# Aligning the heads of four instruction streams to fetch blocks in a single-core decode kernel

## Chip, cores and metric

One core of one Trainium2 chip. The metric is the device time of one execution in microseconds (us); before the change it was 437.0 us, the median of three runs (436.9 to 437.09). Engines are named as in the profile: PE (TensorE), DVE (VectorE), ACT (ScalarE), POOL (GpSimd), SP (SyncE). A fetch is here a packet on one of the DMA queues that the profile marks "instruction" (16 KB or 8 KB each in the trace of before), and a fetch block is the piece of an instruction stream that one such packet is taken to carry.

## What the kernel must compute

One decode step of a conditioned transformer block, batch 8, bf16:

```python
mod = silu(c) @ w_mod                                  # c 8x1024, w_mod 1024x6144; six vectors sa ca ga sb cb gb
h = layernorm(x) * (1 + ca) + sa
x = x + ga * attention(h, k_cache, v_cache, wq, wo)    # 32 query heads, 4 KV heads, 8192 keys, head size 128
h = layernorm(x) * (1 + cb) + sb
x = x + gb * (relu(h @ W_gate) * (h @ W_up)) @ W_down  # 1024 -> 3584 -> 1024
```

K and V are 134.2 MB of the 185.6 MB that must be read.

## The kernel before

A small scheduler, `Prog`, collects the operations of each engine with what they read and write, works out the semaphore waits, and emits one instruction stream for each engine. SP issues all large loads into a ring in on-chip memory. DVE and PE run the attention as a hardware loop of eight trips, two tiles of K and V (4 MB each) to a trip; ACT and POOL are unrolled.

```python
def emit(self, nc, engines, sems):
    ...
    def straight(x, ops):                 # code outside the loop
        known, off = state[x]
        for o in ops:
            want = {}
            ...                           # which semaphores, which values
            body(x, o, new)               # the waits, then the instructions

    after = {}
    for x in engines:                     # sp, act, pool, dve, pe
        mine = [i for i, o in enumerate(self.ops) if o["eng"] == x]
        inside = [i for i in mine if self.ops[i]["trip"] is not None]
        after[x] = [self.ops[i] for i in mine if inside and i > inside[-1]]
        straight(x, [self.ops[i] for i in mine if not inside or i < inside[0]])
        ...
    with nc.Fori(0, len(self.trips["pe"]), engines=...):   # DVE and PE only
        ...
```

The operations at the start, shortened:

```python
pump()                                                  # SP: first half of w_mod, 6 MB
for t, src in enumerate((c_rows, x_rows)):              # 16 KB each: c on SP's queue, A_x on ACT's
    P.op("sp" if t == 0 else "act", lambda e, t=t, src=src: e.dma_start(cx[:, t, :], src), ...)
pump()                                                  # SP: second half of w_mod, Wq, ...
P.op("pool", memset identf); P.op("pool", affine_select identf); ...; rsel; ones; qpad; pT; oT; hmT; identb
P.op("pe", matmul rsel x cx)                            # PE's first matmul: waits for c, A_x and rsel
```

and the tail: `lu = down * gate` and `ob = lu + x` on DVE, then two stores of `ob`.

By count of the built program (the trace does not show it), ACT has 73 instructions, POOL 90, DVE 112 and PE 1351; the loop is PE's instructions 306 to 586.

## Time and profile before

| | before |
|---|---|
| time, median of 3 | 437.0 us |
| span in the profile | 435.9 us |
| moved from HBM | 185.63 MB |
| one loop trip (two K and two V tiles) | about 38.7 us |

The first fence is from the page: the DMA engines in 40 equal slices of the span (a digit is the busy share in tenths, 9 is 90% or more; GB/s is what they moved), and the DMA queues with packets, MB and their share of the 16 DMA engines' span.

```profile
span 435.9 us, 3952 instructions
...
DMA  9999999999999999999999999999999999999995
GB/s 367 435 447 436 432 433 433 432 430 433 433 433 433 433 433 433 431 433 433 433 433 433 433 433 433 433 431 433 433 433 433 433 433 433 426 433 444 421 425 233
...
q1 hardware_dynamic: 6848, 185.63, 98.9%
q8 instruction: 5, 0.08, 0.1%
...
q14 instruction: 3, 0.02, 0.0%
```

The DMA engines are busy throughout, and one queue, q1, which carries the loads, has nearly all of it. The queues marked "instruction" are read here as the fetches of instruction blocks: five packets of 16 KB on q8 and three of 8 KB on q14. The single packet records of the trace put them at 46.2, 86.5, 389.5, 401.9 and 429.8 us (16 KB, 0.88 to 0.95 us each) and at 86.7, 177.6 and 292.8 us (8 KB, 0.31 us each).

Next, the start in order of time (start, duration, engine, line, operation; in brackets the idle time before and what ended it). "SPq" and "ACTq" are issues of loads.

```profile
0.51 0.42 SPq L409 DMA_DIRECT2D cx<-in_c_dram  x1
0.73 0.20 POOL L419 MEMSET identf<- 128x128 f32 x1 [0.29 <-POOLq L812]
0.75 0.39 ACTq L409 DMA_DIRECT2D cx<-in_A_x_dram  x1
...
1.16 1.28 ACT L439 ACT_TABLE_LOAD   x1 [1.16 <-PEq L812]
...
17.69 0.60 PE L435 MATMUL ps<-cx,rsel 32*128 32x512 bf16 x1 [17.69 <-DMA cx<-in_c_dram]
```

ACT issues A_x at 0.75 us and goes on to its table load at 1.16. PE's first matmul waits until c has landed, 17.69 us.

The windows view gives for each stretch its length, the busy time of each engine with the number of instructions, the granted PE clock, the DMA share and GB/s. The first row is the time just before the loop, with Wq arriving; the second is a loop trip.

```profile
core 0: us, PE busy (x) PEld busy (x) DVE busy (x) ACT busy (x) POOL busy (x), PEclk, DMA share, GB/s
...
36.00:48.00 12.00, 3.45 (x32) 0.58 (x16) 2.34 (x5) 0.00 (x0) 0.00 (x0) 0.72 0.97 419
...
100.70:139.40 38.70, 28.11 (x141) 12.40 (x138) 29.75 (x40) 2.56 (x6) 1.64 (x8) 0.85 1.00 434
```

Last, a row of the view of waits (who waited for what: us in total, times, longest).

```profile
DVE kt L575 <- DVEq L180: 30.6, 16, 2.8
```

L575 is the transpose of K, and L180 is the wait ahead of it. All 16 of these waits are at the first transpose of a K tile.

### The profile page before, as it was taken

To read this page: it belongs to the slowest core of one execution; us is meant where nothing else is said; L and a number is where in the kernel's file an instruction comes from. 1 tells how busy PE (TensorE), PEld (TensorE's weight loads), DVE (VectorE), ACT (ScalarE), POOL (GpSimd) and SP (SyncE) were. 2 spreads that over 40 slices of the span, in tenths; PEclk is the share of its full clock that TensorE was granted. 3 is DMA by queue.
4 is the path that set the end of the run, shared out by engine and by line. 5 is a ranking of instruction groups with operands and counts; after the bars stand their busy time and mean duration, and the time that the engine had idled before them with its cause. 6 is when DMAs were issued, how large, how long until landed. Compare 5 with 4: busy or idle time off the path is not lost.

```text
span 435.9 us, 3952 instructions
## 1 busy us (share of the span) xinstructions
PE 275.6 (63%) x1697; PEld 120.4 (28%) x1537; DVE 265.4 (61%) x376; ACT 30.7 (7%) x65; POOL 20.9 (5%) x79
## 2 busy tenths in 40 slices
PE   0063248668595957759595866859595785656336
PEld 0010012323242332324242332324233232352005
DVE  0233048678686877777696867868687777233020
ACT  1100020010101011010101011010101101010000
POOL 7000010000000000000000000000000000000000
PEclk9997658698887889697896969888798969666858
DMA  9999999999999999999999999999999999999995
GB/s 367 435 447 436 432 433 433 432 430 433 433 433 433 433 433 433 431 433 433 433 433 433 433 433 433 433 431 433 433 433 433 433 433 433 426 433 444 421 425 233
DMA packets 6936, 185.76 MB, mean 426 GB/s; under 512 B 816, under 2 KB 912, under 8 KB 1168
## 3 DMA queue, kind: packets, MB, share of 16 engines
q1 hardware_dynamic: 6848, 185.63, 98.9%
q8 instruction: 5, 0.08, 0.1%
q10 hardware_dynamic: 80, 0.02, 0.0%
q14 instruction: 3, 0.02, 0.0%
HBM read 185.63 MB, written 0.02 MB: 426 GB/s over the span
## 4 chain that ended last, share of the span: by engine, by line
PE 46%; DVE 20%; issue 13%; DMA 7%; ACT 0%; SPq 0%
PE ps L634 21%; PE ps L586 18%; DVE kt L575 9%; DMA arena<-in_B_W_down_dram 7%; DVE negm L598 5%; PE ps L604 2%; PE ps L651 2%; PE ps L762 1%; PE ps L731 1%; DVE om L645 1%; DVE mj L609 1%; DVE mjt L612 1%; DVE negm L602 1%; DVE kt L721 0%; DVE lx L693 0%
## 5 line engine op out<-in xcount | busy, mean ns | idle before, releaser
L575 DVE STREAM_TRANSPOSE kt<-arena 128x1024 uint32<-128x1024 uint32 x128 | 149.6, 1217 | 36.8 <-DVEq L180 30.6
L586 PE MATMUL ps<-kt,qpad 128*128 128x512 bf16 x512 | 121.8, 384 | 9.5 <-DVE kt L575 8.2
L634 PE MATMUL ps<-arena,pT 128*64 128x512 bf16 x512 | 93.1, 543 | 50.8 <-issue 50.8
L634 PEld LDWEIGHTS ps<-arena,pT 128*64 128x64 bf16 x512 | 44.9, 155 | 92.8 <-issue 87.5
L586 PEld LDWEIGHTS ps<-kt,qpad 128*128 128x128 bf16 x512 | 45.8, 97 | 83.9 <-DVE kt L575 30.1
L625 DVE STREAM_TRANSPOSE pT<-prb 64x1024 bf16<-64x1024 bf16 x32 | 39.7, 1239 | 16.7 <-ACT prb L618 16.1
L618 ACT ACTIVATE prb<-ps,bias 128x1024 bf16<-128x1024 f32 x16 | 17.8, 1114 | 286.8 <-DVE mjt L612 286.8
L598 DVE TENSOR_REDUCE negm<-ps 128x1 f32<-128x512 f32 x32 | 22.1, 692 | 12.2 <-PE ps L586 12.2
L568 POOL COPY qpad<-qR 32x32 bf16<-32x32 bf16 x64 | 13.1, 204 | 307.7 <-DVE mjt L612 254.3
L762 PE MATMUL ps<-arena,hT 128*32 128x448 bf16 x128 | 12.3, 570 | 10.8 <-DMA arena<-in_B_W_up_dram 5.5
L645 DVE SCALAR_TENSOR_TENSOR om<-ps,im,om 128x128 f32<-128x128 f32 x51 | 17.7, 347 | 0.7
L651 PE MATMUL ps<-jmp,om 128*128 128x16 f32 x34 | 6.9, 280 | 17.0 <-DVE om L645 17.0
L604 PE MATMUL ps<-identf,negm 128*128 128x128 f32 x32 | 7.8, 326 | 15.6 <-DVE negm L602 15.6
L522 PE MATMUL ps<-arena,hT 128*32 128x512 bf16 x64 | 7.1, 620 | 14.6 <-DMA arena<-in_A_wq_dram 14.6
L769 DVE TENSOR_TENSOR kt<-ps,kt 128x448 bf16<-128x448 f32 x2 | 1.2, 620 | 22.0 <-PE ps L762 22.0
L781 PE MATMUL ps<-arena,hmT 128*32 128x256 bf16 x112 | 8.2, 307 | 6.1 <-DMA arena<-in_B_W_down_dram 6.1
L437 DVE CAST cxr<-ps 128x512 bf16<-128x512 f32 x1 | 0.7, 693 | 18.3 <-PE ps L435 18.3
L435 PE MATMUL ps<-cx,rsel 32*128 32x512 bf16 x1 | 0.6, 604 | 17.7 <-DMA cx<-in_c_dram 17.7
L532 DVE CAST kt<-ps 128x512 bf16<-128x512 f32 x1 | 0.7, 692 | 18.1 <-PE ps L522 18.1
L604 PEld LDWEIGHTS ps<-identf,negm 128*128 128x128 f32 x32 | 4.7, 186 | 23.5 <-DVE negm L602 23.5
L651 PEld LDWEIGHTS ps<-jmp,om 128*128 128x128 f32 x34 | 5.3, 195 | 20.5 <-DVE om L645 20.5
L781 PEld LDWEIGHTS ps<-arena,hmT 128*32 128x32 bf16 x112 | 6.0, 109 | 9.2 <-DMA arena<-in_B_W_down_dram 8.1
(88 smaller groups left out, 98.2 us busy)
## 6 DMA issues: line engine op xcount, KB each, us to landing
arena<-in_A_k_cache_dram SPq DMA_DIRECT2D x16, 4096.0 KB, 25.0
arena<-in_A_v_cache_dram SPq DMA_DIRECT2D x16, 4096.0 KB, 20.7
arena<-in_w_mod_dram SPq DMA_DIRECT2D x2, 6144.0 KB, 24.2
arena<-in_A_wq_dram SPq DMA_DIRECT2D x2, 4096.0 KB, 30.6
arena<-in_A_wo_dram SPq DMA_DIRECT2D x2, 4096.0 KB, 23.1
arena<-in_B_W_gate_dram SPq DMA_DIRECT2D x2, 3584.0 KB, 20.9
arena<-in_B_W_up_dram SPq DMA_DIRECT2D x2, 3584.0 KB, 23.3
arena<-in_B_W_down_dram SPq DMA_DIRECT2D x1, 3584.0 KB, 23.7
```

Of the source, the lines that this page charges most:

```text
L568: P.op("pool", lambda e, n=2 * m + Q // 2, Q=Q: e.tensor_copy(qpad[32 * Q:32 * Q + 32, m % 2, :, 24 + 32 * Q:32 + 32 * Q], qR[32 * Q:32 * ...
L575: P.op("dve", lambda e: e.transpose(ktb[:, to:to + QE].bitcast(dt.uint32), arena[:, lo:lo + QE].bitcast(dt.uint32)), reads=[slot_r(lo, lo ...
L586: fns.append(lambda e, t=t, r=r: e.matmul(ps[:, b, :].rearrange("p (c k) -> p c k", k=32), qpad[:, m % 2, t * 2 + r, 24 - 8 * i:152 - 8 * ...
L598: P.op("dve", lambda e: e.tensor_reduce(negm[:, h:h + 1], ps[:, b, :], AX.X, ALU.max, negate=True), reads=[bank(b)] + (free(("v", m - 1)) ...
L604: P.op("pe", lambda e: e.matmul(ps[:, 4, 0:128], negm[:, 2:3].to_broadcast([128, 128]), identf[:], start=True, stop=True), reads=[R("negm" ...
L618: P.op("act", lambda e: e.activation(prb[:], ps[:, 2 * z:2 * z + 2, :].rearrange("p h n -> p (h n)"), ACT.Exp, bias=bias[:, z:z + 1], scal ...
L625: P.op("dve", lambda e, g=g: e.transpose(pT[64 * g:64 * g + 64, z, :, g, :], prb[64 * g:64 * g + 64, :]), reads=[R("prb"), R("pT", z, z + ...
L634: fns.append(lambda e, t=t: e.matmul(ps[64 * (t % 2):64 * (t % 2) + 64, 5, :].rearrange("p (i d) -> p i d", d=Dh), pT[:, z, t].rearrange(" ...
L645: P.op("dve", lambda e, i=i: e.scalar_tensor_tensor(out=om[:], in0=ps[:, 5, Dh * i:Dh * i + Dh], scalar=im[:, i:i + 1], in1=om[:], op0=ALU ...
L651: P.op("pe", lambda e: e.matmul(ps[:, 6 + z, 0:16], om[:], jmp[:].rearrange("p g j -> p (g j)"), start=True, stop=True), reads=[R("om"), R ...
L762: fns.append(lambda e, w=w, r=kk - r0, kk=kk, h=h, j=j, b0=b0: hold(e.matmul(ps[32 * j:32 * j + 32, b0 + h, 0:H], hT[:, kk, :], w[:, r, j, ...
L781: fns.append(lambda e, w=w, r=k - r0, k=k, i2=i2, j=j: e.matmul(ps[32 * j:32 * j + 32, 4, 0:256], hmT[:, k, 1 - i2:33 - i2], w[:, r, i2, j ...
```

## The change

```diff
--- before.py
+++ after.py
@@ -20,6 +20,7 @@
 
     ENGINES = ("sp", "act", "pool", "dve", "pe")
     LOOPED = ("dve", "pe")
+    ALIGNED = dict(act=128, pool=128, dve=128, pe=256)
     N_DMA_SEMS = 20
 
     def __init__(self):
@@ -59,7 +60,7 @@
         self.segs[name] = out
         return covered
 
-    def op(self, eng, fns, reads=(), writes=(), dma=False, own=None, own_wait=None):
+    def op(self, eng, fns, reads=(), writes=(), dma=False, own=None, own_wait=None, page=False):
         if callable(fns):
             fns = [fns]
         i = len(self.ops)
@@ -77,7 +78,7 @@
                 if s[2] is not None and not readers:
                     deps.add((s[2], "waw"))
                 s[2], s[3] = i, []
-        o = dict(eng=eng, fns=fns, writes=list(writes), deps=deps, dma=None, own=own, own_wait=own_wait,
+        o = dict(eng=eng, fns=fns, writes=list(writes), deps=deps, dma=None, own=own, page=page, own_wait=own_wait,
                  trip=self.trip if eng in self.LOOPED else None)
         if dma:
             o["dma"] = self.n_dma
@@ -191,6 +192,10 @@
         def straight(x, ops):
             known, off = state[x]
             for o in ops:
+                if o["page"]:
+                    name = "page_%d" % len(pages)
+                    engines[x].br(name).branch_hint(pages.pop())
+                    nc.switch_bb(name)
                 want = {}
                 for d in o["waits"]:
                     p = self.ops[d]
@@ -203,7 +208,12 @@
                 body(x, o, new)
 
         after = {}
+        pages = []
         for x in engines:
+            if x in self.ALIGNED:
+                engines[x].addr_align(self.ALIGNED[x], offset=0, max_nops=0)
+            if x == "pe":
+                pages.extend(engines[x].mark_branch_hint_location() for o in self.ops if o["page"])
             mine = [i for i, o in enumerate(self.ops) if o["eng"] == x]
             inside = [i for i in mine if self.ops[i]["trip"] is not None]
             after[x] = [self.ops[i] for i in mine if inside and i > inside[-1]]
```

No operation of this kernel passes `page=True`, so those hunks emit nothing. What is left is one `addr_align` on each of four engines; the profile counts four instructions more, 3956 instead of 3952, and the trace of the change has one branch more on each: at 0.69 us on POOL, 0.73 on ACT, 0.76 on DVE and 0.82 on PE.

## The prediction

> What bounds the kernel now. A stream of 185.63 MB from HBM. The page's slices show the DMA engines nine tenths busy or more in 39 of 40 slices, and queue q1 has 98.9% of their span; the windows view gives a DMA share of 1.00 and 432 to 434 GB/s in each loop trip from 62 to 333 us. 185.63 MB at 433 GB/s is 428.7 us; the rest of the 435.9 us is the start, the small last loads (351 GB/s from 424 to 432 us) and 3.5 us after the last weights land. In a trip PE is busy 28.1 of 38.7 us, DVE 29.8, and DVE still waits about 2 us per half trip for K (L575 in the waits view, 30.6 us over 16). The 3.17 us "issue" waits before the PV matmuls are no fetch stalls: the exp (1.1 us) and two transposes of p (2.5 us) run in them.

> What the change does. The `page` hunks are dead: no op passes page=True. What is left is one alignment, with a branch, on ACT, POOL, DVE (128 instructions) and PE (256), at the head of the kernel's own code. No compute, wait or data load changes; instruction fetches move. As built before, ACT has 73 instructions, POOL 90, DVE 112, PE 1351: aligned, the first three fit one block each, PE six. The trace shows fetch packets after the start: five of 16 KB for PE (46, 86, 390, 402, 430 us, about 0.93 us each) and three of 8 KB (87, 178, 293 us, 0.31 us each), all overlapped. They fit PE boundaries at its instructions 192, 448, 704, 960, 1216; after: 256, 512, 768, 1024, 1280. The loop (306 to 586) lies over two blocks before and after, and later trips refetch nothing, so there is nothing to gain in it. [...] at worst a fetch of 2 to 4 us (estimate: PE's packets come about 3 us after its crossing).

> Critical path. Even 4 us at the start is hidden: PE's first matmul waits for c until 17.7 us; POOL is done at 8.7; A_x, issued by ACT at 0.75, lands at 10.1. Wq matmuls wait 6.9 us for data, and Wq half 2 (issued at 32) and K (35) are issued some 6 us before the queue would run dry. One more 16 KB packet costs one DMA engine about 0.6 us at 27 GB/s (433/16, estimate): 0.0 to +0.6 us. The last PE packet moves from 430 to about 432 us, beside the last W_down loads: some tenths at most.

> Predicted: 437.1 us, 436.4 to 438.0 in 8 of 10; faster by over 2%: 0.01, within 2%: 0.97, slower by over 2%: 0.02.

> Right if: trips keep 38.7 us and 433 GB/s; the 8 KB packets of 87, 178 and 293 us are gone or at the very start; PE's packets move by a quarter block; PE's first matmul still waits for c near 17.7 us; POOL's and ACT's first instructions come 0.1 to 4 us later. Wrong if: the branch delays DMA issues so that the queue runs dry before 60 us; the loop's new position makes PE or DVE refetch in every trip (14 or more extra packets and a gap over the 2 us slack); or a fetch stalls PE or DVE after 432 us, where nothing hides it.

The forecast of 437.1 us is before's 437.0 us with the term for one more fetch packet (0.0 to +0.6 us) and at most some tenths for the last one. The branch was no term of the sum: the text counts up to 4 us at the start as hidden.

## The result

| | before | after |
|---|---|---|
| median, 6 runs each | 437.13 us | 437.34 us |
| range | 436.9 to 446.54 | 437.28 to 437.46 |
| ratio of fast runs, after over before | | 1.0005, 95% interval 0.9992 to 1.0019 |

A ratio here and below is the mean time of one kernel's fast runs over the mean of the other's fast runs of the same rounds, so it is not quite the ratio of the medians. The one run of before at 446.5 us counts as slow and is left out of it. The time is the same.

The same lines of the page after:

```profile
span 436.0 us, 3956 instructions
...
DMA  9999999999999999999999999999999999999995
GB/s 378 404 445 433 433 431 436 436 433 428 433 433 436 433 433 433 436 433 433 433 433 433 433 433 433 433 433 433 433 436 433 433 433 433 424 443 425 431 420 244
...
q1 hardware_dynamic: 6848, 185.63, 98.9%
q8 instruction: 6, 0.10, 0.1%
...
q14 instruction: 4, 0.02, 0.0%
```

The packet records show what moved. PE's fetches now come at 5.5, 61.3, 104.1, 390.3, 403.0 and 430.8 us: one more than before, and the others at new places. The three 8 KB fetches in mid-run are gone, and three appear at 5.64, 5.71 and 5.76 us. (The page counts four packets on q14; the fourth is one of 96 bytes at 0.15 us, which just fell inside the span.)

The start after (the change adds ten lines, so L409 of before is L419 here):

```profile
0.51 0.42 SPq L419 DMA_DIRECT2D cx<-in_c_dram  x1
...
1.15 0.20 POOL L429 MEMSET identf<- 128x128 f32 x1 [0.71 <-POOLq L822]
1.17 6.87 ACTq L419 DMA_DIRECT2D cx<-in_A_x_dram  x1
...
8.07 1.28 ACT L449 ACT_TABLE_LOAD   x1 [8.07 <-issue]
...
19.42 0.60 PE L445 MATMUL ps<-cx,rsel 32*128 32x512 bf16 x1 [19.42 <-DMA cx<-in_c_dram]
```

Three things are new. POOL starts 0.42 us later (1.15 instead of 0.73 us), and so does ACT. ACT's issue of A_x, though, takes 6.87 us instead of 0.39, so that its table load comes at 8.07 us. And c, which SP issued at the same time as before, lands 1.7 us later, which moves PE's first matmul from 17.69 to 19.42 us.

In the windows, the loop trip is as it was, and the stretch before the loop has the same DMA share within 0.02 (columns as before):

```profile
36.00:48.00 12.00, 4.17 (x44) 0.58 (x16) 3.39 (x7) 0.60 (x1) 0.00 (x0) 0.72 0.99 429
...
100.70:139.40 38.70, 28.06 (x142) 12.47 (x140) 29.39 (x40) 2.56 (x6) 1.62 (x8) 0.85 1.00 432
```

The first K tile is issued at 36.61 us instead of 34.88, but the third at 75.80 instead of 76.11, and the loop's first transpose starts at 62.75 us, against 62.68 before: the 1.7 us were gone before the loop began.

These three novelties leave three questions: what held ACT for nearly 7 us, what made c late, and whether the stream of loads really hides both and whatever the change might do inside the loop.

### The profile page after: what moved, and what is told of

It is laid out like the page before. It is cut to its first block, busy times and chain, and to the rows that moved or that the text cites. A ratio compares the mean times of both kernels' runs of the same rounds, so it can differ in the third digit from the quotient of the medians.

```text
span 436.0 us, 3956 instructions
## 1 busy us (share of the span) xinstructions
PE 275.4 (63%) x1697; PEld 120.6 (28%) x1537; DVE 263.3 (60%) x376; ACT 30.7 (7%) x65; POOL 20.8 (5%) x79
## 3 DMA queue, kind: packets, MB, share of 16 engines
q1 hardware_dynamic: 6848, 185.63, 98.9%
HBM read 185.63 MB, written 0.02 MB: 426 GB/s over the span
## 5 line engine op out<-in xcount | busy, mean ns | idle before, releaser
L644 PE MATMUL ps<-arena,pT 128*64 128x512 bf16 x512 | 91.9, 538 | 50.8 <-issue 50.8
L635 DVE STREAM_TRANSPOSE pT<-prb 64x1024 bf16<-64x1024 bf16 x32 | 39.7, 1239 | 16.7 <-ACT prb L628 16.1
L628 ACT ACTIVATE prb<-ps,bias 128x1024 bf16<-128x1024 f32 x16 | 17.8, 1113 | 286.2 <-DVE mjt L622 286.2
L655 DVE SCALAR_TENSOR_TENSOR om<-ps,im,om 128x128 f32<-128x128 f32 x51 | 17.7, 347 | 0.7
L532 PE MATMUL ps<-arena,hT 128*32 128x512 bf16 x64 | 7.2, 631 | 12.8 <-DMA arena<-in_A_wq_dram 12.8
L445 PE MATMUL ps<-cx,rsel 32*128 32x512 bf16 x1 | 0.6, 602 | 19.4 <-DMA cx<-in_c_dram 19.4
```

The source lines that it names most:

```text
L628: P.op("act", lambda e: e.activation(prb[:], ps[:, 2 * z:2 * z + 2, :].rearrange("p h n -> p (h n)"), ACT.Exp, bias=bias[:, z:z + 1], scal ...
L635: P.op("dve", lambda e, g=g: e.transpose(pT[64 * g:64 * g + 64, z, :, g, :], prb[64 * g:64 * g + 64, :]), reads=[R("prb"), R("pT", z, z + ...
L644: fns.append(lambda e, t=t: e.matmul(ps[64 * (t % 2):64 * (t % 2) + 64, 5, :].rearrange("p (i d) -> p i d", d=Dh), pT[:, z, t].rearrange(" ...
L655: P.op("dve", lambda e, i=i: e.scalar_tensor_tensor(out=om[:], in0=ps[:, 5, Dh * i:Dh * i + Dh], scalar=im[:, i:i + 1], in1=om[:], op0=ALU ...
```

## Experiments

Twelve runs were made, one of them (start_later5_again) a repetition. The two that load only half of most K and V tiles compute on stale data: the check did not notice that. Short fences show A_x's issue, ACT's first table load and PE's first matmul, in that form of the timeline.

| run | median us | ratio to before (95% interval) |
|---|---|---|
| act_only | 437.52 | 1.0006 (0.9985 to 1.0028) |
| pe_only | 436.73 | 0.9995 (0.9977 to 1.0013) |
| act_after_x | 437.06 | 1.0005 (0.9987 to 1.0023) |
| x_late | 437.32 | 1.0017 (0.9997 to 1.0038) |
| act_x_at_8 | 436.99 | 0.9997 (0.9981 to 1.0014) |
| start_later5 | 439.00 | 1.0039 (0.9979 to 1.0099) |
| start_later5_again | 437.82 | 0.9997 (0.9964 to 1.0029) |
| start_later12 | 443.01 | 1.0122 (1.0076 to 1.0169) |
| half_plain | 430.88 | 0.9829 (0.9778 to 0.9879) |
| half_aligned | 430.57 | 0.9831 (0.9787 to 0.9875) |
| tail_one | 437.53 | 1.0012 (0.9995 to 1.0028) |
| tail_three | 442.49 | 1.0124 (1.0107 to 1.0141) |

The medians include slow runs (one of act_only, one of start_later5_again); the ratios do not. By the rule of 2% the verdict is "same" for all but the two half runs, which are "unclear"; start_later12 and tail_three are slower all the same, by 1.2%, with intervals clear of 1.

### act_only: ScalarE alone is aligned

```diff
-    ALIGNED = dict(act=128, pool=128, dve=128, pe=256)
+    ALIGNED = dict(act=128)
```

> Only ScalarE is aligned. After the change ScalarE issued A_x at 1.17 us, that issue took 6.87 us, the table load came at 8.07 and A_x landed 7.5 us later than before; c landed on a few engines 1.7 us late. If ScalarE's own branch causes all this, this run shows the same: issue of A_x near 1.2 us, about 6.9 us long, table load at 8 us. If the fetches of the other engines (PE's 16 KB above all) cause it, ScalarE shows only the branch of 0.4 us and A_x lands near 10 us. Time under both theories within 0.3% of before (about 437.2 us), because data loads bound the kernel.

```profile
1.17 5.92 ACTq L419 DMA_DIRECT2D cx<-in_A_x_dram  x1
...
7.12 1.28 ACT L449 ACT_TABLE_LOAD   x1 [7.12 <-issue]
...
18.04 0.60 PE L445 MATMUL ps<-cx,rsel 32*128 32x512 bf16 x1 [18.04 <-DMA cx<-in_c_dram]
```

In this run ACT's own branch is enough: the issue comes at 1.17 us and takes 5.92 us. One 8 KB fetch packet came at 5.53 us, and the one that before had at 292.8 us is missing, so that one was ACT's. c is late by 0.35 us only (18.04 instead of 17.69). That is small but outside the scatter: in the five profiles with c undisturbed (before, x_late, half_plain, tail_one, tail_three) this matmul starts between 17.57 and 17.72 us.

### pe_only: TensorE alone is aligned

```diff
-    ALIGNED = dict(act=128, pool=128, dve=128, pe=256)
+    ALIGNED = dict(pe=256)
```

> Only TensorE is aligned. One 16 KB fetch packet near 5 us; six such packets in all. If this packet delays c on a few DMA engines, c lands near 19.4 us instead of 17.7; if the late A_x packets of ScalarE's queue do, c lands at 17.7 us. A_x is issued at 0.75 us and lands near 10. Time within 0.3% of before.

```profile
0.75 0.39 ACTq L419 DMA_DIRECT2D cx<-in_A_x_dram  x1
...
1.16 1.28 ACT L449 ACT_TABLE_LOAD   x1 [1.16 <-PEq L822]
...
18.48 0.60 PE L445 MATMUL ps<-cx,rsel 32*128 32x512 bf16 x1 [18.48 <-DMA cx<-in_c_dram]
```

ACT is as before. PE's fetches came at 5.3, 61.2, 103.6, 390.1, 402.7 and 430.4 us, so the q8 packets are PE's. c is late by 0.79 us with nothing else changed: here one more 16 KB fetch packet ahead of it goes with the whole delay. c's 32 packets of 512 bytes show where: 28 of them started between 16.25 and 16.6 us, the last four at 17.4 to 17.7. After the full change 20 of the 32 started by 16.6 us and the last 12 between 16.85 and 18.62. So some of c's packets lag, read here as those of a few of the 16 DMA engines, and PE's first matmul waits for the last of them: of c's 16 landing signals the last came at 17.64 us in before, and after the change the last five came at 18.17 to 19.37 us, with the matmul at 19.42. The expectation of 19.4 us for this run was too high: only the kernels in which all four engines fetch come to 19 us or more (19.02 in act_after_x, 19.42 in the change, 19.61 in half_aligned).

### act_after_x: ScalarE branches after it has issued A_x

```diff
-    ALIGNED = dict(act=128, pool=128, dve=128, pe=256)
+    ALIGNED = dict(pool=128, dve=128, pe=256)
...
-  lambda e: e.dma_start(cx[:, t, :], src)
+  lambda e: (e.dma_start(cx[:, t, :], src), t == 1 and e.addr_align(128, offset=0, max_nops=0))[0]
```

> All four engines are aligned as in the change, but ScalarE branches after it has issued A_x. Theory fetch (ScalarE stands still until its block has come): A_x lands near 10 us, but the table load still comes at 6 to 8 us. Theory order (the issue of A_x is held up because it now comes after the issue of the second half of w_mod at 0.98 us): the issue at 0.75 us takes 0.4 us, and the table load follows within 1 us of it. Time within 0.3% of before either way.

```profile
0.74 0.39 ACTq L419 DMA_DIRECT2D cx<-in_A_x_dram  x1
...
1.58 1.28 ACT L451 ACT_TABLE_LOAD   x1 [1.58 <-SPq L824]
...
19.02 0.60 PE L447 MATMUL ps<-cx,rsel 32*128 32x512 bf16 x1 [19.02 <-DMA cx<-in_c_dram]
```

The issue takes 0.39 us and the table load comes at 1.58 us, 0.42 us later than before: the price of the branch here. It did not wait until 6 to 8 us, as the simple fetch theory had it: that theory falls. c is still late (19.02 us, 1.33 more than before), as the fetch packets are still there (q8 has six, as in the change). The other 0.40 us of the change's 1.73 come only with the late A_x; whether they are its doing or scatter, no run separates.

### x_late: no alignment, A_x issued after the second half of w_mod

```diff
-for t, src in enumerate((c_rows, x_rows)):
+for t, src in enumerate((c_rows,)):
...
 P.op("pool", lambda e: aff(e, identf[:], 0, [[-1, 128]]), ...)
+P.op("act", lambda e: e.dma_start(cx[:, 1, :], xsrc), reads=[R("identf")], ...)
```

> No alignment at all; ScalarE's A_x load waits for GpSimd's identity, ready at 1.5 us, so that it is issued after the second half of w_mod. Theory order: the issue takes about 7 us again and the packets of A_x come after 12 us. Theory fetch: it takes 0.4 us and A_x lands near 10 to 11 us. Time within 0.3% of before.

```profile
1.50 0.39 ACTq L422 DMA_DIRECT2D cx<-in_A_x_dram  x1
...
1.92 1.28 ACT L441 ACT_TABLE_LOAD   x1 [1.92 <-POOL rsel L424]
...
17.68 0.60 PE L437 MATMUL ps<-cx,rsel 32*128 32x512 bf16 x1 [17.68 <-DMA cx<-in_c_dram]
```

Issued at 1.50 us, after the second half of w_mod, the load still took 0.39 us to issue. So the order theory falls as well. With no fetch at the start, c landed as before.

Both first theories are out. What is left, as a theory, is that it needs both: a branch that has just set off a fetch, and then a DMA issue.

### act_x_at_8: ScalarE aligned, A_x issued after the fetch has landed

```diff
-    ALIGNED = dict(act=128, pool=128, dve=128, pe=256)
+    ALIGNED = dict(act=128)
...
 P.op("pool", lambda e: e.memset(oT[:], 0.0), ...)
+P.op("act", lambda e: e.dma_start(cx[:, 1, :], xsrc), reads=[R("oT")], ...)
```

> ScalarE alone is aligned, and its A_x load, still the first instruction of the new block, waits for a GpSimd memset that ends near 7.4 us, after the fetch packet of 5.5 us has landed. Theory overlap (an issue of a DMA right after the branch is held until the fetch that the branch set off is done): the issue now takes 0.4 us and A_x lands near 17 us. Rival, place (the first DMA issue in a new block is slow whenever it comes): it takes 6 us again, from 7.5 to 13.5 us. Time within 0.3% of before in both.

```profile
7.46 0.39 ACTq L439 DMA_DIRECT2D cx<-in_A_x_dram  x1
7.88 1.28 ACT L451 ACT_TABLE_LOAD   x1 [7.88 <-POOL oT L438]
...
18.07 0.60 PE L447 MATMUL ps<-cx,rsel 32*128 32x512 bf16 x1 [18.07 <-DMA cx<-in_c_dram]
```

The fetch packet came at 5.74 us. The issue at 7.46 us, still the first instruction of the new block, took 0.39 us. So in this run the place in the block did no harm, and the overlap is what differs: in the three runs in which ACT's DMA issue followed right behind the branch, it was done 1.25 to 1.97 us after the end of the 8 KB packets (act_only: packet until 5.84 us, issue done at 7.09; the change: packets until 6.07, issue done at 8.04; half_aligned: until 5.87, done at 7.76). Which of the three packets is ACT's cannot be told where several engines fetch, and PE's 16 KB packet ran until 6.78 us in the change. Why the issue took so long was not seen, and that it is the fetch, and not some other work of the branch that lasts as long, is inferred from these times. What the runs show is that ACT's issue right behind the branch took 5.92 us (act_only), 6.60 (half_aligned) and 6.87 us (the change), and one before the branch (act_after_x), a later one (act_x_at_8) or one without a branch (x_late) took 0.39.

### start_later5, start_later5_again and start_later12: how much delay the start hides

None of the three has an alignment. Memsets put off the time at which POOL has the first matmul's weights ready.

```diff
+for _ in range(6):        # start_later12: range(8)
+    P.op("pool", lambda e: e.memset(pT[:], 0.0), reads=[R("pT", 0, 2)], writes=[R("pT", 0, 2)])
 P.op("pool", lambda e: e.memset(rsel[:], 0.0), ...)
...
-P.op("pool", lambda e: e.memset(pT[:], 0.0), ...)
```

> Before's kernel without alignment; five more GpSimd memsets make the first matmul's weights ready near 23 us instead of 2, so that TensorE's first matmul runs about 5 us later than the 17.7 us of before, three times the delay that the change brings. Slack theory: the DMA queue still holds Wq's first half until about 41.7 us when its second half is issued (32 + 5 = 37 us), so the time stays within 0.3% of before (437.1 us). Rival, the start lies on the critical path: about +5 us, 442 us.

> The same with seven more memsets: the first matmul runs about 12 us later, near 30 us. Slack theory: Wq's second half is issued near 44 us[...], and the queue ran dry at about 41.7 us: a gap of 3 to 5 us in the stream, and +3 to +5 us in the time (440 to 442 us). Rival, the start lies on the critical path: +12 us, 449 us. If the time does not move at all, the kernel is not bound by the stream as I read it.

Its gap of 3 to 5 us is 44 less 41.7, or 2.3 us, and a term for the time from the issue to the first data; before's first load took 1.0 us from issue (0.08 us) to first packet (1.09).

start_later5, PE's first matmul and the loop's first transposes:

```profile
23.34 0.58 PE L436 MATMUL ps<-cx,rsel 32*128 32x512 bf16 x1 [23.34 <-POOL rsel L424]
...
63.04 1.25 DVE L576 STREAM_TRANSPOSE kt<-arena 128x1024 uint32<-128x1024 uint32 x1 [2.77 <-DVEq L180]
```

The first matmul came 5.65 us later than before, and the loop 0.36 us (63.04 against 62.68). Two of the four timed runs were at 437.5 to 437.7 us, two at 440.3 to 440.6, and a run of before in the same rounds was at 440.1, so the ratio's interval, 0.9979 to 1.0099, was too wide to decide. It was run again in five rounds:

> A repetition, in more rounds, of the start made 5.6 us later, because two of its four runs were at 440.5 us and two at 437.5 us, and one run of before in the same rounds was at 440.1 us too. Slack theory: within 0.3% of before (ratio 0.997 to 1.003), since the profile showed the loop's first transpose only 0.36 us later. Rival, the delay costs something after all: a ratio of 1.006 or more with an interval above 1.

0.9997 (0.9964 to 1.0029): no cost of a 5.6 us delay is seen, and one above 1.3 us is ruled out (0.0029 x 437). The few runs near 440 us, with the change and without it, stay unexplained. The change's 1.7 us are well inside the delay tested.

start_later12's window of 36 to 48 us, to be read against 0.97 and 419 GB/s in the fence of before:

```profile
36.00:48.00 12.00, 8.43 (x100) 2.02 (x36) 3.64 (x14) 0.49 (x2) 0.00 (x0) 1.00 0.51 205
```

The first matmul came at 30.48 us, 12.8 later. Now the second half of Wq was issued at 45.1 us, when the queue had run dry: the DMA share of that window is 0.51, which is 5.5 us less DMA work than before ((0.97 - 0.51) x 12). The time rose by about 5.3 us (0.0122 x 437; interval 3.3 to 7.4), near the 3 to 5 us expected. The slack at the start is therefore about 7.5 us (12.8 - 5.3; 5.4 to 9.5), and what exceeds it is paid. That rules out both rivals: a start that costs its whole delay, and a stream that does not matter.

### half_plain and half_aligned: the loop without the stream

From the third pair on, only half of each K and V tile is loaded; all the arithmetic remains, on stale data.

```diff
+part = n // 2 if key[0] in "kv" and key[1] > 1 else n
-P.op("sp", lambda e, dst=dst, src=src: e.dma_start(dst, src), ...)
+P.op("sp", lambda e, ...: e.dma_start(dst[:, 0:part] if part < n else dst, src[:, 0:part] if part < n else src), ...)
```

> Wrong result on purpose: from the third pair of K and V tiles on, only half of each tile is loaded, the arithmetic is unchanged. 126.9 MB remain, 293 us at 433 GB/s, so the compute bounds the loop. Expected trip: 37 us or less instead of 38.7, whole time 410 to 430 us. It is the base for half_aligned.

> The changed kernel with the same half loads: the loop is bound by compute, so what the new position of the loop in the fetch blocks costs or gains per trip is no longer hidden by the stream. Theory: the position changes nothing, the trips agree with half_plain within 0.1 us and the times within 0.3%. Rival: the crossing costs something in each trip that the stream hid; then the trips differ by 0.2 us or more and the times by 1.5 us or more.

A loop trip of half_plain, then the same window of half_aligned (columns as in the windows above):

```profile
100.70:139.40 38.70, 28.10 (x142) 12.56 (x140) 30.48 (x41) 2.56 (x6) 1.63 (x8) 0.85 0.62 243
```

```profile
100.70:139.40 38.70, 28.11 (x142) 12.54 (x140) 30.34 (x41) 2.56 (x6) 1.62 (x8) 0.85 0.62 242
```

The stream runs at 243 GB/s, where before had 434, and yet the trips hardly got shorter. K tiles were issued from 75.74 to 327.65 us in half_plain, 13 tiles in 251.91 us or 38.76 us for two; in before it was 76.11 to 328.46, or 38.82. The expected 37 us or less was wrong. The whole time fell by only 1.7%. And the row of waits for the transposes of K:

```profile
DVE kt L578 <- PE ps L589: 30.6, 15, 2.9
```

The total is again 30.6 us, but it is not the same wait. Here is one K tile (the eighth) in before, then in half_plain; a tile has eight transposes, and `x4` is a run of four:

```profile
198.10 4.63 DVE L575 STREAM_TRANSPOSE kt<-arena 128x1024 uint32<-128x1024 uint32 x4 [1.93 <-DVEq L180]
203.69 2.37 DVE L575 STREAM_TRANSPOSE kt<-arena 128x1024 uint32<-128x1024 uint32 x2 [0.96 <-PE ps L586]
```

```profile
195.41 4.63 DVE L578 STREAM_TRANSPOSE kt<-arena 128x1024 uint32<-128x1024 uint32 x4
202.89 2.37 DVE L578 STREAM_TRANSPOSE kt<-arena 128x1024 uint32<-128x1024 uint32 x2 [2.86 <-PE ps L589]
```

In before the tile landed at 197.97 us and the first transpose started at 198.10: DVE waited for K. In half_plain the tile had landed at 179.60, the first transpose did not wait, and the fifth waited longer for PE to be done with earlier transposed K (there are four buffers for it). Over all tiles, DVE idled 30.6 us before first and 6.2 us before fifth transposes in before, and 5.8 and 30.6 us in half_plain: 36.8 and 36.4 us together. So the wait for K was real, but ending it gains nothing, because DVE then waits for PE instead: the loop has a chain of compute of its own that is as long as the stream. That the two totals are both 30.6 is chance; in the other profiles with all loads the wait for K sums to 30 to 41 us.

For the change this made the test sharper, because in half_aligned the loads leave the DMA engines idle for over a third of the trip above (share 0.62, 242 GB/s), so that little can hide behind them. Its K issues run from 76.31 to 328.60 us: 38.81 us for two tiles, 0.06 us more than half_plain (0.15%), the whole times 430.57 and 430.88 us. To within these differences, the new position of the loop in the fetch blocks neither costs nor gains. No fetch packet fell between 105 and 388 us in half_aligned, as none fell between 104.1 and 390.3 us in the change: the later trips of the loop, some 280 instructions on PE, left no fetch packet.

### tail_one and tail_three: a branch where nothing hides it

Before's kernel, with alignments on DVE alone, after the first of the last two operations.

```diff
-P.op("dve", lambda e: e.tensor_tensor(out=lu[0:64, :], ...), ...)
+P.op("dve", lambda e: (e.tensor_tensor(out=lu[0:64, :], ...), e.addr_align(128, offset=0, max_nops=0))[0], ...)
     # tail_three: addr_align(256, 0), addr_align(256, 128), addr_align(256, 0) in a row
```

> Before's kernel with one alignment to 128 on VectorE alone, between the last two additions of the tail (after the gate multiply, before the final add), where nothing hides a stall. The branch cost GpSimd and ScalarE about 0.42 us at the start; here it may overlap the 0.42 us multiply. If the next block is already there, the gap between the two instructions grows by 0 to 0.4 us and the time by no more (437.0 to 437.5 us). If a branch to the next block has to wait for a fetch, the gap grows by 3 to 6 us (440 to 443 us).

> The same place, but three alignments in a row (to 256, to 128 past it, to 256 again)[...]. If such a branch waits for a fetch: two more 8 KB packets at the end, a gap of 3 to 10 us, time 440 to 447 us. If fetches never stall: a gap of about 1.2 us (three branches of 0.42), time near 438 us.

Neither text says what its 3 to 6 and 3 to 10 us are worked out from. Of the runs before them, the change shows 4.7 to 5.1 us from a branch (PE 0.82; POOL, ACT and DVE 0.69 to 0.76 us) to the start of the fetch packets (16 KB at 5.48, 8 KB at 5.64 to 5.76).

The two operations in before, in tail_one and in tail_three:

```profile
433.37 0.42 DVE L785 TENSOR_TENSOR lu<-ps,xg 64x256 f32<-64x256 f32 x1 [11.29 <-PE ps L781]
433.82 0.42 DVE L787 TENSOR_TENSOR ob<-lu,xg 64x256 bf16<-64x256 f32 x1
```

```profile
433.27 0.42 DVE L785 TENSOR_TENSOR lu<-ps,xg 64x256 f32<-64x256 f32 x1 [11.29 <-PE ps L781]
433.85 0.42 DVE L788 TENSOR_TENSOR ob<-lu,xg 64x256 bf16<-64x256 f32 x1 [0.15 <-DVE lu L785]
```

```profile
433.25 0.42 DVE L785 TENSOR_TENSOR lu<-ps,xg 64x256 f32<-64x256 f32 x1 [11.29 <-PE ps L781]
438.93 0.42 DVE L788 TENSOR_TENSOR ob<-lu,xg 64x256 bf16<-64x256 f32 x1 [5.27 <-issue]
```

From start to start they stand 0.45 us apart before, 0.58 with one branch and 5.68 with three. The one branch cost 0.13 us here, behind a running instruction; its fetch packet came at 434.4 us, when the next instruction had already started (433.85), so that one did not wait for it. The three branches left fetch packets at 434.6, 437.0 and 439.5 us: the first two fall inside the gap of 5.27 us (433.67 to 438.93), which therefore reads as two waits of about 2.5 us (an estimate: half the gap is 2.6 us, and the packets lie 2.4 and 2.5 us apart), and the whole 5.4 us (0.0124 x 437) is in the time.

## Why the prediction was right, point by point

The time, 437.34 us, lies within 436.4 to 438.0, and "within 2%" was right. The steps did not all hold.

- *"The `page` hunks are dead"*: right; the streams differ by one alignment instruction on each of four engines.
- *Fetches move; PE's boundaries go to 256, 512, 768, 1024, 1280*: right in kind. The 8 KB packets went to the start, PE has six packets instead of five, and the last came at 430.8 us (said: about 432). "PE's packets move by a quarter block" was not borne out: the one in the loop moved by 17.7 us, where a quarter block (64 of some 280 instructions in 38.7 us) is 8.8 us on average, and the last three by only 0.8 to 1.1. The boundaries themselves are not in the trace, so their exact places stay open.
- *What a branch costs*: measured, 0.42 us at the start (POOL's first own memset at 1.15 us instead of 0.73) and 0.13 us behind an instruction (tail_one). Three branches in a row left 5.27 us of idle time (tail_three), by estimate two waits of about 2.5 us.
- *"at worst a fetch of 2 to 4 us"* and *"POOL's and ACT's first instructions come 0.1 to 4 us later"*: POOL's first instruction and the start of ACT's came 0.42 us later, but the bound failed for ACT. Its table load came 6.9 us later, because the DMA issue behind the branch took 6.87 us instead of 0.39 and was done after the fetch packets. This used up all of A_x's slack: its landing signals came at 16.7 to 17.8 us instead of 9.5 to 10.2. The last of them is later than c's last in before (17.64 us), and only because c came later still (19.37) did it not matter. That this did not show even at the first matmul was luck, not foreseen; the slack of the start, tested to 5.6 us, would have covered so small a delay in any case.
- *"PE's first matmul still waits for c near 17.7 us"*: failed by 1.7 us. That one more fetch packet takes a DMA engine's time was in the prediction, as an estimate of 0.6 us on the whole time, but not that c comes later with it: its last landing signal came at 19.37 us instead of 17.64. Measured: +0.35 us with one 8 KB packet (and A_x late), +0.79 with one 16 KB packet, +1.33 with all four, +1.73 with all four and A_x late.
- *"Even 4 us at the start is hidden ... some 6 us before the queue would run dry"*: right, and now measured: 5.6 us hidden, 12.8 us cost 5.3. This is the step that carried the forecast.
- *"DVE still waits about 2 us per half trip for K"*: right (the first transposes start 0.14 us after K's landing). Counting on it as slack (*"a gap over the 2 us slack"*) was not safe: with half the K and V bytes a trip lasts 38.76 instead of 38.82 us, and the idle time moves to a wait for PE. That the DMA never idles in the loop is true (share 1.00), so the stream does set the time, but the compute chain is as long to 0.2%. A cost on that chain would have had no 2 us to hide in; no run put one there. This did not hurt the forecast because the change costs nothing in the loop that half_aligned shows (0.06 us a trip).
- *A last packet beside the W_down loads, some tenths at most*: consistent, not shown; the difference of the medians, 0.2 us, is within the interval.

So the change is neutral for two separate reasons: within the loop it changes nothing to within 0.06 us a trip (half_aligned), and at the start it costs 1.7 us that the backlog of loads absorbs (start_later5). The fetches that it moved had no cost to save that the time shows. No kernel that loads all of K and V beat before by more than its interval, so no better version is offered.

## What to carry to other kernels

Look for fetch packets on the instruction queues that fall inside an idle stretch of an engine on the critical path, as two did in the 5.27 us of tail_three, the one place of this case where the whole time rose with fetches (5.4 us); if there are none, this case gives no sign that alignment has anything to win. If streams are aligned at their heads all the same, issue the first loads before the branch, as act_after_x does (0.39 us for the issue), since here a load just behind it took 5.92 to 6.87 us to issue. And before a wait for a load is counted as slack, take the load away: a shorter stream with the same arithmetic shows whether the compute chain is just as long. Then compare single instructions and landings: two equal totals in the view of waits, 30.6 us here, were two different waits.
